# A second junk buffer for the squares of a set-attention and SoLU kernel

## The chip, the cores and the metric

One core of one Trainium2 chip. The metric is the device time of one launch in microseconds; lower is better. The engines are named as the profile names them: PE (TensorE, matmuls; PEld its weight loads), DVE (VectorE), ACT (ScalarE), POOL (GpSimd), SP (SyncE, which issues the DMAs).

## The reference

`x` has 4 sets of 12608 tokens of 128 channels. An attention with 32 inducing points makes `h` per set, a second one lets the tokens attend to `h`; its 50432 rows then go through a feed-forward part of width 1024:

```python
def mab(q, kv):
    s = scale * (q @ kv.transpose(0, 2, 1))
    a = np.exp(s - s.max(-1, keepdims=True))
    a /= a.sum(-1, keepdims=True) + 1e-09
    return a @ kv
h = mab(I, x)
out = mab(x, h)
...
h = x @ w_in
e = np.exp(h - np.max(h, axis=-1, keepdims=True))
solu = h * (e / (np.sum(e, axis=-1, keepdims=True) + 1e-09))
mu, var = mean(solu), mean((solu - mu) ** 2)
ln = (solu - mu) / np.sqrt(var + 1e-06) * g_ln
return ln @ w_out
```

## The kernel before

The tokens of a set are cut into tiles of 128, four to a group, 396 tiles in all. A tile of the feed-forward part runs through `soft` (L1337): PE has put the 1024 columns of `h` into PSUM (L1276, L1306), DVE copies them, scaled by the attention's norm, into a buffer `hn` and takes their extreme (L1349); ACT takes the exponential into a buffer `eu` and its sum into a column of `qe` (L1360); POOL multiplies the two in place, which gives solu without its norm (L1364, 2.37 us each); then two engines read `eu`: ACT squares it for the variance (`square`, L1373 to L1382, its instruction on L1375), and DVE transposes it in blocks into `vt` (L1391). PE multiplies `vt` by the output weights in a stream of small matmuls (`emit` in `products`, L1551), DVE or ACT moves the sums out of PSUM (`evacuate`, L1580), and `finish` (L1605 to L1630) turns the sums into the norm and scales the rows. Pieces of one tensor, `spare`, serve as further buffers for `hn`, `eu` and results, so some rows name `spare` where others name `eu` or `hn`.

The square's 128x1024 result is needed by nobody: only its sum is, which the instruction hands to a column of `qe` as its accumulated output (a second record in the trace, ACTIVATION_READ_ACCUMULATOR). The result itself goes to a junk buffer in bf16, `sq` (L340), one for the whole kernel. A buffer `eu` is free again when its square and its transposition are both done.

A planner written in Python (`Planner`, `Op`, costs in ns, priorities such as `PR_SQ`) sets the order of each engine's instructions at build time. It knows nothing of waits on `sq`: the cost it takes for a square is 1040 ns, whatever stands ahead. Each engine then works its list in that order. The framework adds the waits: every ACT instruction counts up one semaphore, shown as Activation_49; an instruction that writes what an earlier one has written or read waits for that count, also on its own engine. A wait that an earlier wait of the same engine already covers is left out. An instruction holds one wait; for a second one an EVENT_SEMAPHORE instruction is put ahead of it.

Of the kernel before, what the change touches and what calls it, by code (L numbers as in the profile page):

```python
# [10 lines left out]
BF16 = mybir.dt.bfloat16  # L11
U32 = mybir.dt.uint32
I32 = mybir.dt.int32
AF = mybir.ActivationFunctionType
# [5 lines left out]
P = 128  # L20
C = 128
M = 32
FF = 1024
# [16 lines left out]
OS_LATE = 2000  # L40
SLOTS = 3
STRETCH = 20
JS = [
# [56 lines left out]
PR_SQ = 6  # L100
# [59 lines left out]
class Planner:  # L160
# [8 lines left out]
    def spawn(self, gen, prio):  # L169
        self._step([gen, prio, 0], None)  # L170
# [8 lines left out]
    def give(self, lock, buf, *after):  # L179
        lock.free.append((buf, after))  # L180
        while lock.free and lock.waiting:
            lock.waiting.sort(key=lambda w: (w[2], w[1]))
            task = lock.waiting.pop(0)[0]
            self.blocked -= 1
            self._step(task, lock.free.pop(0))
# [69 lines left out]
    def run(self):  # L255
        clock = self.clock
        while self.ops:
            first = min(self.ops, key=lambda o: (max(clock[o[0].eng], o[1]), o[3]))
            eng = first[0].eng
            limit = max(clock[eng], first[1]) + self.slack[eng]  # L260
            stretch = int(limit / 1000 / STRETCH)
            wide, turn = JS[stretch] if stretch < len(JS) else (0, 0)
            pick = min(
# [20 lines left out]
def set_attention_then_solu_kernel(ctx: ExitStack, tc: tile.TileContext, x, inducing, w_in, w_out, g_ln, out):  # L284
    nc = tc.nc
    NB, N, _ = x.shape
    scale = 1.0 / float(C) ** 0.5
# [27 lines left out]
    def buf(shape, name, dtype=F32, where=None):  # L315
        return (where or const).tile(shape, dtype, name=name)

    def bufs(n, shape, name, dtype=F32):
        return [buf(shape, f"{name}{i}", dtype) for i in range(n)]
# [17 lines left out]
    where = bank_pool.__enter__()  # L337
    bank_e = [buf([P, 512], f"bank_e{i}", where=where) for i in range(8)]
    hn_b = bufs(3, [P, FF], "hn")
    sq = buf([P, FF], "sq", BF16)  # L340

    eu_b = buf([P, EUS, FF], "eu")
    xT_b = buf([C, PG, P], "xT")
# [996 lines left out]
    def soft(t, b, j, s, hp, d):  # L1340
        G = grp[(b, j)]
        ka, i = part_of[b, ff_groups[j][0] + s]
        A = aT_of[(b, ka)]
        hn, rel = yield HN
        nm, mrel = yield NM
        rn = A["aT"][1][:, i : i + 1]
        d = yield Op(
            "DVE", 1208,
            lambda: nc.vector.tensor_scalar(out=hn, in0=hp, scalar1=rn, scalar2=None, op0=ALU.mult, op1=ALU.min, accum_out=nm),  # L1349
            d, rel, mrel, prio=t + PR_HN,  # L1350
        )
        give(H, hp, d)
        give(TURN, None, d)
        A["left"] -= 1
        if not A["left"]:
            give(AT, A["aT"], d)
        srel = yield G["st"]
        e, rel = yield EU
        de = yield Op(
            "ACT", 1133, lambda: nc.scalar.activation(e, hn, AF.Exp, bias=nm, scale=-1.0, accum_out=G["qe"][:, s, 1:2]), d, rel, srel,  # L1360
            prio=t + PR_EX,
        )
        give(NM, nm, de)
        d = yield Op("POOL", 2330, lambda: nc.gpsimd.tensor_tensor(out=e, in0=hn, in1=e, op=ALU.mult), de, prio=t + PR_MU)  # L1364
        give(HN, hn, d)
        left = []

        def over(d):
            left.append(d)
            if len(left) == 2:  # L1370
                give(EU, e, *left)

        def square():  # L1373
            ds = yield Op(
                "ACT", 1040, lambda: nc.scalar.activation(sq, e, AF.Square, scale=1.0 / 32.0, accum_out=G["qe"][:, s, 0:1]), d,  # L1375
                prio=t + PR_SQ,
            )
            G["squared"].append(ds)
            over(ds)
            if (b, j) != final and len(G["squared"]) == ff_groups[j][1]:  # L1380
                yield from floor(b, j)

        spawn(square(), t)
        n = ff_groups[j][1]
        rel = yield G["vt"]
        if (b, j) == final:
            yield from straight(t, b, j, s, e, d, rel, over)
            return
        dt = yield Op(
            "DVE", 1163,  # L1390
            lambda: nc.vector.transpose(  # L1391
                out=G["vtb"][:, : n * FF].rearrange("p (j s t) -> p j s t", j=M, s=n)[:, :, s, :],
                in_=e.rearrange("p (a f) -> p a f", f=M),
            ),
            d, rel, prio=t + PR_TU,
        )
        over(dt)
        G["turned"].append(dt)
        if len(G["turned"]) == n:
            for w in range(2):  # L1400
                spawn(products(b, j, t, w), t)

    def floor(b, j):
        G = grp[(b, j)]
        n = ff_groups[j][1]
        flat = G["dd"][: P * 2 * n].rearrange("(p f) -> p f", f=2 * n)
        ds = yield dma(
            P * 8 * n, lambda: nc.sync.dma_start(flat, G["qe"][:, :n, :].rearrange("p s v -> p (s v)")), G["squared"], prio=-30, issue=600
        )
        f, i = fin_of[b, j]  # L1410
        F = fin[(b, f)]
        rel = yield F["buf"]
        dl = F["dl"][:, 4 * i : 4 * i + 4, :]
        laid = G["dd"][: P * 2 * n].rearrange("(a t s v) -> s t a v", a=4, t=M, v=2)
        dealt = []
        for s in range(n):
            d = yield dma(P * 8, lambda: nc.sync.dma_start(dl[s * M : (s + 1) * M], laid[s]), ds, rel, prio=-30, issue=600)
            dealt.append(d)
        plan.set(G["floor"], *dealt)
        give(ST, G["stb"], *dealt)  # L1420
# [14 lines left out]
    def straight(t, b, j, s, e, d, vrel, over):  # L1435

        G = grp[(b, j)]
        f, _ = fin_of[b, j]
        F = fin[(b, f)]
        uT = G["vtb"].rearrange("p (s k t) -> p s k t", s=GS, k=KC)[:, s]  # L1440
        tr, rel = yield H.at(OP_FIRST + t)

        def turn():
            for k in range(KC):
                nc.tensor.transpose(out=tr[:, k * P : (k + 1) * P], in_=e[:, k * P : (k + 1) * P], identity=ident)

        d = yield Op("PE", SWITCH + 108.7 * KC, turn, d, rel, prio=t - 60)
        over(d)
        half = KC // 2
        view = tr.rearrange("p (k t) -> p k t", k=KC)  # L1450
        halves = []

        def part(eng, cost, fn, k0):
            dc = yield Op(eng, cost, lambda: fn(uT[:, k0 : k0 + half], view[:, k0 : k0 + half]), d, vrel, prio=t - 60)
            halves.append(dc)
            if len(halves) == 2:
                plan.set(turned_both, *halves)

        turned_both = Event()
        spawn(part("ACT", 510, nc.scalar.copy, 0), t - 60)  # L1460
        spawn(part("DVE", 620, nc.vector.tensor_copy, half), t - 60)
        got = yield turned_both
        give(H, tr, *got)
        wrel = yield w_full_ready
        bank, rel = yield H.at(OP_FIRST + t)

        def add():
            for k in range(KC):
                nc.tensor.matmul(bank[:, : C + 1], lhsT=uT[:, k], rhs=w_full[0][:, k], start=(k == 0), stop=(k == KC - 1))

        d = yield Op("PE", SWITCH + 225 * KC, add, got, rel, wrel, prio=t - 55)
        rel = yield F["buf"]
        d = yield Op("ACT", 190, lambda: nc.scalar.copy(F["raw"][:, s, :], bank[:, : C + 1]), d, rel, prio=t - 60)
        give(H, bank, d)
        F["out"].append(d)
        F["left"] -= 1
        if not F["left"]:
            spawn(last_finish(b, j, f), -100)
# [282 lines left out]
```

## Time and profile before

| | before |
|---|---|
| median of 3 runs (lowest to highest) | 1186.43 us (1186.13 to 1186.9) |
| the profiled execution's own time | 1184.99 us |
| its span, first to last instruction | 1183.1 us |
| granted TensorE clock, mean | 0.996 |
| squares on ACT (L1375) | 329 + 67 |

Times and busy shares are of one profiled execution. A row of the time line gives an instruction's start in us from the span's start, its length in us, engine, line, operation, what it writes and reads, its shape, and how many such instructions in a row it stands for. An instruction of ACT may start before the record ahead of it has ended.

### The profile page before, as it was taken

What the parts mean: (1) busy time and instruction counts of PE and PEld (TensorE: products, weight loads), DVE (VectorE), ACT (ScalarE), POOL (GpSimd) and SP (SyncE); (2) the same over time, 40 slices, a digit from 0 to 9 for tenths busy, and PEclk for the clock granted to TensorE, in tenths of its full rate; (3) what the DMA queues carried; (4) which work ended last, traced back from release to release, by engine and by line L of the source; (5) the groups of instructions that cost most, each with busy time, mean ns of one, the idle gap of its engine ahead of it and who ended that gap; (6) DMA issues with size and microseconds to landing.
All of it is one profiled execution on the core that took longest, in us unless ns stands there. A gap on an engine that the chain in (4) does not pass through costs nothing.

```text
span 1183.1 us, 67935 instructions
## 1 busy us (share of the span) xinstructions
PE 1147.1 (97%) x30537; PEld 1050.5 (89%) x30537; DVE 1073.7 (91%) x1628; ACT 1115.4 (94%) x2193; POOL 1064.2 (90%) x619
## 2 busy tenths in 40 slices
PE   9899999999999999999999999999999999999996
PEld 7568999998999898989899989999899989899896
DVE  6899999998999899999999899999999998999891
ACT  4799999999999999999999999999999999999994
POOL 2488899988998999989899899899999999999995
PEclk9999999999999999999999999999999999999999
DMA  9632332432144333423122354242313132120203
GB/s 337 238 118 75 111 111 76 136 96 67 25 117 119 108 111 110 129 81 100 40 58 83 96 147 151 75 126 61 84 40 84 41 80 67 31 65 4 49 5 88
DMA packets 167108, 110.62 MB, mean 93 GB/s; under 512 B 78336, under 2 KB 132000, under 8 KB 166688
## 3 DMA queue, kind: packets, MB, share of 16 engines
q1 hardware_dynamic: 166816, 106.27, 31.1%
q8 instruction: 239, 3.92, 1.4%
q14 instruction: 53, 0.43, 0.1%
HBM read 53.51 MB, written 52.17 MB: 89 GB/s over the span
## 4 chain that ended last, share of the span: by engine, by line
PE 39%; ACT 31%; POOL 11%; issue 7%; DVE 7%; DMA 3%; SPq 0%; ACTq 0%; DVEq 0%; POOLq 0%
PE h L1551 30%; ACT sq L1375 12%; ACT eu L1360 11%; POOL eu L1364 8%; PE h L1306 3%; ACT spare L1360 2%; POOL spare L1364 2%; DVE vt L1391 2%; DVE spare L1349 2%; ACT spare L1580 1%; DVE hn L1349 1%; POOL spare L1626 1%; ACT a L1048 1%; ACT xT L700 1%; PE h L688 1%
## 5 line engine op out<-in xcount | busy, mean ns | idle before, releaser
L1551 PE MATMUL h<-wc,vt 32*128 32x129 f32 (+1 forms) x25344 | 986.7, 273 | 12.9 <-ACT spare L1580 7.9
L1551 PEld LDWEIGHTS h<-wc,vt 32*128 32x128 f32 (+1 forms) x25344 | 954.9, 184 | 44.7 <-ACT spare L1580 17.5
L1364 POOL TENSOR_TENSOR eu<-hn,eu 128x1024 f32<-128x1024 f32 x166 | 392.7, 2373 | 26.9 <-ACT eu L1360 25.7
L1306 PE MATMUL h<-hs,aT 32*128 32x512 f32 x1528 | 404.9, 602 | 4.9 <-DVE hn L1349 1.4
L1391 DVE STREAM_TRANSPOSE vt<-eu 128x1024 f32<-128x1024 f32 x326 | 398.3, 1231 | 12.1 <-POOL eu L1364 11.1
L1364 POOL TENSOR_TENSOR eu<-spare,eu 128x1024 f32<-128x1024 f32 x163 | 385.7, 2373 | 19.4 <-ACT eu L1360 19.2
L1375 ACT ACTIVATE sq<-eu 128x1024 bf16<-128x1024 f32 x329 | 345.6, 1050 | 13.9 <-POOL eu L1364 5.8
L1349 DVE TENSOR_SCALAR_CACHE_REDUCE hn<-h,rn 128x1024 f32<-128x1024 f32 x201 | 253.2, 1261 | 21.6 <-PE h L1306 10.1
L1349 DVE TENSOR_SCALAR_CACHE_REDUCE spare<-h,rn 128x1024 f32<-128x1024 f32 x195 | 245.7, 1263 | 22.4 <-PE h L1306 9.6
L1360 ACT ACTIVATE eu<-hn,nm 128x1024 f32<-128x1024 f32 x166 | 189.1, 1139 | 1.9 <-DVE hn L1349 1.3
L1360 ACT ACTIVATE eu<-spare,nm 128x1024 f32<-128x1024 f32 x163 | 185.9, 1141 | 2.2 <-DVE spare L1349 1.8
L1306 PEld LDWEIGHTS h<-hs,aT 32*128 32x128 f32 x1528 | 121.7, 185 | 22.2 <-issue 3.9
L1364 POOL TENSOR_TENSOR spare<-spare 128x1024 f32<-128x1024 f32 x32 | 75.9, 2371 | 9.2 <-ACT spare L1360 8.9
L1391 DVE STREAM_TRANSPOSE vt<-spare 128x1024 f32<-128x1024 f32 x66 | 81.4, 1233 | 2.6 <-POOL spare L1364 2.5
L1364 POOL TENSOR_TENSOR spare<-hn,spare 128x1024 f32<-128x1024 f32 x35 | 83.0, 2372 | 0.0
L1626 POOL TENSOR_TENSOR spare<-spare,fin 128x512 f32<-128x512 f32 x79 | 79.7, 1039 | 1.6
L1375 ACT ACTIVATE sq<-spare 128x1024 bf16<-128x1024 f32 x67 | 70.3, 1049 | 1.9 <-POOL spare L1364 0.3
L1375 ACT ACTIVATION_READ_ACCUMULATOR sq<-eu 128x1 f32 x329 | 61.8, 188 | 0.0
L688 PE MATMUL h<-ident,xn 32*128 32x32 f32 x1124 | 51.4, 224 | 0.9 <-issue 0.6
L1580 ACT COPY spare<-h 128x774 f32<-128x774 f32 (+3 forms) x69 | 45.0, 654 | 6.0 <-PE h L1551 4.0
L688 PEld LDWEIGHTS h<-ident,xn 32*128 32x128 f32 x1124 | 49.0, 136 | 1.3 <-issue 0.8
L1360 ACT ACTIVATE spare<-hn,nm 128x1024 f32<-128x1024 f32 x35 | 39.9, 1140 | 0.1
(200 smaller groups left out, 935.7 us busy)
## 6 DMA issues: line engine op xcount, KB each, us to landing
out_dram<-spare SPq DMA_DIRECT2D x95, 256.0 KB, 3.1
xT<-xd SPq DMA_DIRECT2D x93, 256.0 KB, 3.9
xn<-in_x_dram SPq DMA_DIRECT2D x75, 256.0 KB, 3.8
xd<-xT SPq DMA_DIRECT2D x72, 256.0 KB, 2.7
dl<-dd SPq DMA_DIRECT2D x392, 1.0 KB, 2.7
xd<-vt SPq DMA_DIRECT2D x7, 768.0 KB, 7.9
spare<-in_x_dram SPq DMA_DIRECT2D x15, 256.0 KB, 7.6
wc<-in_x_dram SPq DMA_DIRECT2D x6, 256.0 KB, 4.1
```

Source lines behind the costliest of these rows:

```text
L688: nc.tensor.transpose(out=tr[:, k * 512 + s * M : k * 512 + (s + 1) * M], in_=xn[r, s, :], identity=ident[r, r])
L700: lambda: nc.scalar.copy(xT.rearrange("c s (q t) -> c q s t", q=4)[:, 2 * w : 2 * w + 2, :n, :], tr.rearrange("c (k x) -> c k x", k=2)[:, ...
L1048: de = yield Op("ACT", 90 + 54 * n, lambda: nc.scalar.activation(a4[:, :n], twice, AF.Exp, scale=scale), d, arel)
L1306: nc.tensor.matmul(hp[:, cols], lhsT=aT[rows, i // 2, :], rhs=hs[rows, cols], start=True, stop=True)
L1349: lambda: nc.vector.tensor_scalar(out=hn, in0=hp, scalar1=rn, scalar2=None, op0=ALU.mult, op1=ALU.min, accum_out=nm),
L1360: "ACT", 1133, lambda: nc.scalar.activation(e, hn, AF.Exp, bias=nm, scale=-1.0, accum_out=G["qe"][:, s, 1:2]), d, rel, srel,
L1364: d = yield Op("POOL", 2330, lambda: nc.gpsimd.tensor_tensor(out=e, in0=hn, in1=e, op=ALU.mult), de, prio=t + PR_MU)
L1375: "ACT", 1040, lambda: nc.scalar.activation(sq, e, AF.Square, scale=1.0 / 32.0, accum_out=G["qe"][:, s, 0:1]), d,
L1391: lambda: nc.vector.transpose(out=G["vtb"][:, : n * FF].rearrange("p (j s t) -> p j s t", j=M, s=n)[:, :, s, :], in_=e.rearrange("p (a f) ...
L1551: nc.tensor.matmul(op[:rows, a - 2 * w, :], lhsT=vt[q, k, :], rhs=wc[q, k, :], start=(k == 0), stop=(k == JB - 1))
L1580: return lambda: eng(to, at)
L1626: return lambda: eng.tensor_tensor(out=raw, in0=raw, in1=y[:, i0 : i0 + 4].unsqueeze(2).to_broadcast([rows, 4, C]), op=ALU.mult)
```

## The change

Two junk buffers `sq0` and `sq1` stand in the place of `sq`, and the squares, in the order in which the planner places them, take them in turn. The planner's cost for a square is the same number under a name. The second buffer takes 2 KB of every partition and lies behind the first, so all tensors allocated later move by 2 KB.

```diff
+SQ_NS = 1040
...
-    sq = buf([P, FF], "sq", BF16)
+    sq_b = bufs(2, [P, FF], "sq", BF16)
+    squares = [0]
...
         def square():
-            ds = yield Op(
-                "ACT", 1040, lambda: nc.scalar.activation(sq, e, AF.Square, scale=1.0 / 32.0, accum_out=G["qe"][:, s, 0:1]), d,
-                prio=t + PR_SQ,
-            )
+            def squared():
+                squares[0] += 1
+                nc.scalar.activation(sq_b[squares[0] % 2], e, AF.Square, scale=1.0 / 32.0, accum_out=G["qe"][:, s, 0:1])
+
+            ds = yield Op("ACT", SQ_NS, squared, d, prio=t + PR_SQ)
```

The instructions of all five engines stand in the same order in both programs, and on PE, DVE, POOL and SP every wait is for the same count of the same semaphore. Only waits of ACT for its own semaphore differ. In the rows that follow, a number behind a tile's name is a running number of the build (`sq_83` is `sq0` and `sq_84` is `sq1` in the changed program), Activation_49 is ACT's own semaphore and Pool_49 that of POOL; line numbers of the changed program are two or three higher.

ACT, the piece of its list that the trace has at 263 to 271 us, before:

```order
L1360 ACTIVATE eu,qe_104<-spare,nm_114 128x1024
L1612 ACTIVATE fin_109<-fin_109 128x20 [waits Pool_49]
L1613 ACTIVATE fin_109<-fin_109 128x20 [waits Activation_49]
L1614 ACTIVATE fin_109<-fin_109 128x20 [waits Activation_49]
L1375 ACTIVATE sq,qe_102<-eu 128x1024
L1375 ACTIVATE sq,qe_104<-eu 128x1024 [waits Activation_49,Pool_49]
L1375 ACTIVATE sq,qe_104<-eu 128x1024 [waits Activation_49]
L1375 ACTIVATE sq,qe_104<-eu 128x1024 [waits Activation_49,Pool_49]
L1618 ACTIVATE fin_109<-fin_109 128x20 [waits Pool_49]
```

The same piece of the changed program:

```order
L1362 ACTIVATE eu,qe_105<-spare,nm_115 128x1024 [waits Activation_49]
L1615 ACTIVATE fin_110<-fin_110 128x20 [waits Pool_49]
L1616 ACTIVATE fin_110<-fin_110 128x20 [waits Activation_49]
L1617 ACTIVATE fin_110<-fin_110 128x20 [waits Activation_49]
L1378 ACTIVATE sq_83,qe_103<-eu 128x1024
L1378 ACTIVATE sq_84,qe_105<-eu 128x1024 [waits Pool_49]
L1378 ACTIVATE sq_83,qe_105<-eu 128x1024 [waits Activation_49]
L1378 ACTIVATE sq_84,qe_105<-eu 128x1024 [waits Activation_49,Pool_49]
L1621 ACTIVATE fin_110<-fin_110 128x20 [waits Pool_49]
```

Nothing moved. Before, the second, third and fourth instruction in a row that squares waits for the count of the square just ahead of it. After, the second square has lost that wait, and the waits for Activation_49 of the third and the fourth are for the square two places ahead, which wrote the same junk buffer. The exponential in the first row has gained a wait for a count that an earlier square's wait covered before.

ACT, the piece at 277 to 281 us, before (the square ahead of the first COPY is the one that the second square waits for):

```order
L1375 ACTIVATE sq,qe_106<-eu 128x1024 [waits Pool_49]
L1580 COPY spare<-h_698 128x2x3x129 [waits PE_49]
L1375 ACTIVATE sq,qe_106<-spare 128x1024 [waits Activation_49,Pool_49]
L1580 COPY spare<-h_696 128x2x3x129 [waits PE_49,Activation_49]
L950 ACTIVATE accn<-acc_128,small_120 128x128 [waits DVE_49]
```

The same piece of the changed program:

```order
L1378 ACTIVATE sq_84,qe_107<-eu 128x1024 [waits Pool_49]
L1583 COPY spare<-h_699 128x2x3x129 [waits PE_49]
L1378 ACTIVATE sq_83,qe_107<-spare 128x1024 [waits Pool_49]
L1583 COPY spare<-h_697 128x2x3x129 [waits PE_49,Activation_49]
L952 ACTIVATE accn<-acc_129,small_121 128x128 [waits DVE_49]
```

Nothing moved here either; the second square has lost a wait for the square two places ahead.

Counted over the whole list of ACT: 142 of the 396 squares stand directly behind another square and wait for it before; 52 of them have that wait alone, 90 have one for POOL too. In the changed program no square waits for the instruction directly ahead of it. Of the 142, 87 wait for a square two or more places ahead and 55 have no wait for ACT left. 65 exponentials that had no wait for ACT's own semaphore have one: 9 of them for the square two places ahead, 56 for one three or more places ahead. 29 exponentials wait for the square directly ahead of them in both programs, since they overwrite the `eu` that it reads.

## Rows read from the trace of the kernel before

**Rows 1.** The page's first lines: span, and busy time of each engine.

```profile
span 1183.1 us, 67935 instructions
PE 1147.1 (97%) x30537; PEld 1050.5 (89%) x30537; DVE 1073.7 (91%) x1628; ACT 1115.4 (94%) x2193; POOL 1064.2 (90%) x619
```

**Rows 2.** Busy time by stretch: us, then busy us by engine with instruction counts.

```profile
core 0: us, PE busy (x) PEld busy (x) DVE busy (x) ACT busy (x) POOL busy (x), PEclk, DMA share, GB/s
...
900.00:1000.00 100.00, 97.04 (x2754) 91.42 (x2750) 96.53 (x128) 97.96 (x190) 98.95 (x55) 1.00 0.22 52
...
1100.00:1160.00 60.00, 57.55 (x1585) 54.88 (x1582) 49.10 (x62) 58.17 (x121) 59.84 (x37) 1.00 0.15 34
...
100.00:1160.00 1060.00, 1040.18 (x28882) 969.76 (x28878) 988.85 (x1436) 1032.27 (x2015) 997.58 (x567) 1.00 0.30 82
```

**Rows 3.** Longest waits of ACT from 100 to 1160 us: us, times, longest us.

```profile
ACT sq L1375 <- POOL eu L1364: 2.6, 8, 0.5
ACT xT L700 <- PE h L688: 2.2, 4, 1.4
```

**Rows 4.** Waits of POOL and of PE's weight loads for ACT, whole span.

```profile
POOL eu L1364 <- ACT eu L1360: 44.9, 36, 5.5
...
PEld h L1551 <- ACT spare L1580: 17.5, 25, 1.7
```

**Rows 5.** The chain that ended last, shares by engine, then by line.

```profile
PE 39%; ACT 31%; POOL 11%; issue 7%; DVE 7%; DMA 3%; SPq 0%; ACTq 0%; DVEq 0%; POOLq 0%
...
by line: PE h L1551 29.8%; ACT sq L1375 12.4%; ACT eu L1360 10.7%; POOL eu L1364 8.3%; issue 7.1%; PE h L1306 3.5%; ACT spare L1360 2.0%; POOL spare L1364 1.9%; DVE vt L1391 1.7%; DVE spare L1349 1.5%; ACT spare L1580 1.4%; DVE hn L1349 1.3
```

**Rows 6.** The chain by line, from 300 to 400, then from 900 to 1000 us.

```profile
by line: PE h L1551 65.1%; PE h L1306 7.3%; ACT eu L1360 7.0%; ACT sq L1375 6.1%; issue 5.2%; PE h L768 2.0%; ACT xT L700 1.9%; PE h L1093 1.3%; ACT spare L1580 1.1%; ACT a L1048 1.0%; PE h L885 0.9%; PE h L688 0.9%; PE h L806 0.6%; ACT spa
...
by line: ACT sq L1375 26.4%; ACT eu L1360 26.3%; issue 12.8%; PE h L1551 7.9%; ACT spare L1360 6.9%; DVE vt L1391 3.6%; DVE spare L1349 3.4%; ACT spare L1580 2.3%; ACT a L1048 1.9%; DMA dl<-dd 1.7%; DMA dd<-qe 1.4%; DVE hn L1349 1.3%; DVE s
```

**Rows 7.** Time line of ACT: a square with no late wait, and four in a row.

```profile
238.62 1.04 ACT L1375 ACTIVATE sq<-eu 128x1024 bf16<-128x1024 f32 x1
239.57 0.19 ACT L1375 ACTIVATION_READ_ACCUMULATOR sq<-eu 128x1 f32 x1
239.66 1.13 ACT L1360 ACTIVATE eu<-hn,nm 128x1024 f32<-128x1024 f32 x1
...
264.90 1.04 ACT L1375 ACTIVATE sq<-eu 128x1024 bf16<-128x1024 f32 x1
265.85 0.19 ACT L1375 ACTIVATION_READ_ACCUMULATOR sq<-eu 128x1 f32 x1
266.13 1.06 ACT L1375 ACTIVATE sq<-eu 128x1024 bf16<-128x1024 f32 x1
...
267.31 1.06 ACT L1375 ACTIVATE sq<-eu 128x1024 bf16<-128x1024 f32 x1
...
268.55 1.06 ACT L1375 ACTIVATE sq<-eu 128x1024 bf16<-128x1024 f32 x1
...
269.61 0.20 ACT L1618 ACTIVATE fin<-fin 128x20 f32<-128x20 f32 x1
```

**Rows 8.** Groups of squares: count, busy us, mean ns, idle us before them.

```profile
L1375 ACT ACTIVATE sq<-eu 128x1024 bf16<-128x1024 f32 x329 | 345.6, 1050 | 13.9 <-POOL eu L1364 5.8
...
L1375 ACT ACTIVATE sq<-spare 128x1024 bf16<-128x1024 f32 x67 | 70.3, 1049 | 1.9 <-POOL spare L1364 0.3
```

**Rows 9.** Time line of ACT: a square with two waits behind a COPY.

```profile
278.91 0.81 ACT L1580 COPY spare<-h 128x774 f32<-128x774 f32 x1
279.62 1.06 ACT L1375 ACTIVATE sq<-spare 128x1024 bf16<-128x1024 f32 x1
```

**Rows 10.** The line L1375 alone: its extra wait instructions, ns min/median/max.

```profile
L1375 ACTq EVENT_SEMAPHORE  x171: 17/17/17, 84.0 to 1163.6; - x171
```

## The prediction

> **What bounds the kernel now.** I read the busy shares first, then the waits, then the chain that ended last, and only then the squares. All four computing engines are nearly full: over the span ACT is busy 94% of the time, DVE 91%, POOL 90%, and PE shows 97% [rows 1]. From 100 to 1160 us, where the feed-forward part runs steadily, ACT is busy 1032.27 of 1060 us, PE 1040.18, POOL 997.58, DVE 988.85 [rows 2]. So the question is which of them sets the pace. The waits say that ACT hardly waits for anyone: its two longest sorts of wait in that stretch come to 2.6 and 2.2 us [rows 3], though it is idle for 1060 - 1032.27 = 27.7 us. The others do wait for ACT: POOL 44.9 us for the exponentials, PE's weight loads 17.5 us for the copies out of PSUM [rows 4]. That idle time of ACT that no other engine ends is the first hint that ACT waits for itself. The chain that ended last runs 39% on PE and 31% on ACT, with POOL at 11% and DVE at 7%; the squares alone hold 12.4% of it [rows 5]. It changes hands: from 300 to 400 us the matmul stream of L1551 holds 65.1%, and from 900 to 1000 us squares and exponentials hold 26.4 + 26.3% [rows 6].
>
> **What a square's wait costs.** The reader should compare starts. A square that is followed by an instruction without a late wait passes the engine on after 239.66 - 238.62 = 1.04 us: the exponential starts 0.10 us before the square's accumulator record has ended (239.57 + 0.19 = 239.76) [rows 7]. In the run of four squares, the second starts at 266.13, which is 0.09 us after the first one's record has ended (265.85 + 0.19 = 266.04); the distances from start to start are 1.23 (two waits), 1.18 (one wait) and 1.24 us (two waits), and the last square takes 269.61 - 268.55 = 1.06 us until L1618 starts [rows 7]. The order of the program says why: each of these squares waits for the count of the one ahead, since both write `sq`. So a wait for the square directly ahead costs 1.18 - 1.04 = 0.14 us where it stands alone and 1.24 - 1.04 = 0.20 us where POOL's wait makes a second one. In both figures 0.02 us is the square's own longer run to its accumulator record, 1.06 us against 1.04.
>
> **The sum on ACT.** 142 squares have such a wait, 52 alone and 90 with a second one: 52 x 0.14 + 90 x 0.20 = 7.3 + 18.0 = 25.3 us of ACT's time. The change takes all 142 away, since the square directly ahead now writes the other buffer. As a check, the profile puts 13.9 + 1.9 us of idle time before squares, and lays only 5.8 + 0.3 us of it to POOL [rows 8]; the rest is the waiting, and the lost overlap is not idle time and so is not in that figure.
>
> **What is added.** 87 of the 142 squares now wait for a square two or more places ahead. A full square of 1.04 us lies between, so that wait should be over before the engine is free. The row that is nearest is a square that in the old program waits for the square two places ahead and for POOL: it starts at 279.62, 0.10 us before the COPY ahead of it ends (278.91 + 0.81 = 279.72) [rows 9]. I cost these at nothing; the cover is the square between. The 65 exponentials that gain a wait for a square two or more places ahead are costed at nothing by the same row; if the cover failed, each would pay between 0.14 and 0.20 us, 9 to 13 us in all. The extra wait instructions take 17 ns each on ACT's sequencer [rows 10] and run ahead of the engine; squares need fewer of them, exponentials more, so the balance is nothing. The order on every engine is unchanged, and no other engine waits for a square except by way of a free `eu` buffer and the small DMAs of the sums, which can only come earlier. The 2 KB move of the later tensors changes no shape and no start within a row; I cost it at nothing.
>
> **What of it reaches the end.** Only squares on the path that sets the end can shorten it. The squares hold 12.4% of 1183.1 us, 146.7 us, of the chain [rows 5], out of 345.6 + 70.3 = 415.9 us that they are busy [rows 8]. So 146.7 / 415.9 = 35% of them lie on the chain, and 0.35 x 25.3 = 8.9 us leave it. The bounds are nothing, if PE or POOL is just as late wherever ACT is on the chain, and 25.3 us, if ACT sets the pace throughout. I take 8.0: the figure of the chain less a tenth, because another path of nearly the same length is late next where the chain changes engines, above all POOL, which is busy 98.95 of 100 us from 900 and 59.84 of 60 us from 1100 [rows 2].
>
> **A rule that speaks against it.** The trace has ACT's next instruction start 0.10 us early without a late wait and 0.09 us late with one [rows 7]. The Trainium skill, VectorE: DVE Perf Modes, section The DRAIN you can't avoid, says of VectorE that its emptying of the pipeline cannot be skipped by leaving out semaphores between operations, and that the semaphore costs nothing extra. By that rule, were it true of ACT, the sum would be nothing. The rows of this trace say otherwise for ACT, so it keeps a small chance, as the third rival.
>
> **The rivals.** First, *ACT sets the pace throughout*. For it: ACT waits so little for others [rows 3], and PE's share of the chain rests on ends of matmuls that the profile models. The whole 25.3 us would come off, less what POOL, full at the end [rows 2], keeps back: 12 to 23 us, about 16, so some 1170 us. Against it: the chain leaves ACT for 69% of the time [rows 5]. The Trainium skill, Perfetto Trace Analysis, section Identifying the Most-Contended Engine, holds matmul busy time to be a poor measure and points to the weight loads; by that reading ACT's 94% would be the highest here, above the weight loads' 89%, which is this rival.
>
> Second, *PE is late next*. If its 1040.18 us are real work, it has 1060 - 1040.18 = 19.8 us left [rows 2], of which 31%, ACT's part of the chain [rows 5], is 6.1 us; some of that PE waits for DVE and for its own issue. A gain of 0 to 4 us, about 2, so some 1184 us. For it: the stretch from 300 to 400 us, where the stream of L1551 holds the chain [rows 6]. Against it: the weight loads' waits for ACT [rows 4], which would shrink.
>
> Third, *a square behind a square cannot start earlier anyway*, because the accumulator record must be out first: no change, 1186.4 us. Against it: the exponential at 239.66, which starts before that record has ended [rows 7], and which writes an accumulator too.
>
> Fourth, on the other side, *the waits move to the exponentials*. If 65 of them pay 0.20 us, that is 13.0 us; exponentials stand ahead of POOL, which waits for them already [rows 4]. Were all of that on the chain and the squares' gain hidden, the result would be 1199 us. It turns slower from 8.9 / 0.20 = 45 late waits on the chain. Against it: the square of [rows 9], and that each of them waits for an instruction at least two places ahead.
>
> **How the numbers follow.** The sum is made against the profiled execution, 1184.99 us with a span of 1183.1 us [rows 1]; the median of the runs is 1.4 us above that, and I subtract from the median: 1186.43 - 8.0 = 1178.4 us. A measurement of this kernel can tell about 0.2%, 2.4 us, from no change. The forecast, a gain of 4 to 12 us, has a chance of 0.60; ACT throughout 0.16; PE next 0.18, of which 0.05 would be within 2.4 us; no earlier start 0.03; the exponentials 0.03. Faster is 0.60 + 0.16 + 0.13 = 0.89, the same 0.05 + 0.03 = 0.08, slower 0.03. The range runs from a gain of 15 us to one of 2 us, 1171.4 to 1184.4 us: it leaves out about 0.06 of the first rival, 0.05 of the second, and the last two, 0.17 together.
>
> **What would show it.** Right: squares in a row start 1.04 us apart, no square takes 1.06 us for that reason, the idle time before squares falls to the part that POOL ends, the exponentials keep their 0.10 us early start, and the new idle time of ACT is put down to PE, DVE or POOL. Starts still 1.18 or more apart would make the price wrong; starts 1.04 apart with the end hardly moved would make the share of the chain wrong, and the rows would then show which engine ACT waits for.

## The result and the profile after

The changed kernel takes 1170.12 us (median of 4 runs, 1169.5 to 1171.28) against 1186.66 us (median of 4 runs, 1186.13 to 1186.93): a ratio of 0.9862 with a 95% interval of 0.9845 to 0.9879. That is 16.5 us less, about twice the forecast, and below the range. Two later comparisons of the same kernel on other occasions gave 0.9879 and 0.9864.

Span and busy time of the profiled execution after (1171.28 us), to set against [rows 1], and its chain that ended last, to set against [rows 5]:

```profile
span 1169.5 us, 67905 instructions
PE 1143.9 (98%) x30537; PEld 1049.5 (90%) x30537; DVE 1071.5 (92%) x1628; ACT 1102.5 (94%) x2193; POOL 1064.1 (91%) x619
...
PE 46%; POOL 20%; ACT 17%; DVE 8%; issue 6%; DMA 3%; SPq 1%; ACTq 0%; DVEq 0%; POOLq 0%
```

ACT's share of the chain fell from 31% to 17%, POOL's rose from 11% to 20%. ACT's busy time fell by 12.9 us: in the lost overlap the square's accumulator record ran with nothing beside it, so it counted as busy ([rows 7]: the record ends at 266.04, the next square starts at 266.13). The rest of what was removed was idle time, as the groups of squares show below.

The time line of ACT after, in the piece of the program that [rows 7] show before:

```profile
262.74 1.04 ACT L1378 ACTIVATE sq<-eu 128x1024 bf16<-128x1024 f32 x1
263.69 0.19 ACT L1378 ACTIVATION_READ_ACCUMULATOR sq<-eu 128x1 f32 x1
263.78 1.04 ACT L1378 ACTIVATE sq<-eu 128x1024 bf16<-128x1024 f32 x1
...
264.82 1.04 ACT L1378 ACTIVATE sq<-eu 128x1024 bf16<-128x1024 f32 x1
...
265.86 1.04 ACT L1378 ACTIVATE sq<-eu 128x1024 bf16<-128x1024 f32 x1
...
266.90 0.20 ACT L1621 ACTIVATE fin<-fin 128x20 f32<-128x20 f32 x1
```

The four squares now start 1.04 us apart and all take 1.04 us; from the first one's start to L1621 it is 4.16 us, where it was 269.61 - 264.90 = 4.71. That is 0.55 us less for one wait of 0.14 and two of 0.20, as priced. The third and fourth still wait for the square two places ahead, and that costs nothing here. What holds for this run of four holds for the list: read over the whole trace, the 52 squares with one wait started at the median 1.17 us after the square ahead and the 90 with two 1.24 us; after the change the median of the 142 is 1.04 us.

The groups of squares after, to set against [rows 8]:

```profile
L1378 ACT ACTIVATE sq<-eu 128x1024 bf16<-128x1024 f32 x329 | 343.7, 1045 | 7.1 <-POOL eu L1366 6.5
...
L1378 ACT ACTIVATE sq<-spare 128x1024 bf16<-128x1024 f32 x67 | 70.0, 1046 | 0.5 <-POOL spare L1366 0.5
```

The line's extra wait instructions after, to set against [rows 10]:

```profile
L1378 ACTq EVENT_SEMAPHORE  x93: 17/17/17, 96.7 to 1147.9; - x93
```

The idle time before squares fell from 13.9 + 1.9 to 7.1 + 0.5 us, and nearly all that is left, 6.5 + 0.5, is ended by POOL. So the part that POOL does not end fell from 9.7 to 0.6 us. With the 12.9 us of busy time that makes 22.0 us, near the 25.3 us priced. The squares need 93 extra wait instructions in place of 171.

Who waited after: ACT for POOL in the steady part (100 to 1150 us), then POOL and the weight loads for ACT over the span, to set against [rows 3, 4]:

```profile
ACT sq L1378 <- POOL eu L1366: 5.4, 14, 1.2
...
POOL eu L1366 <- ACT eu L1362: 38.6, 32, 5.5
...
PEld h L1554 <- ACT spare L1583: 12.5, 21, 1.3
```

Busy time by stretch after, with the columns of [rows 2]:

```profile
900.00:1000.00 100.00, 98.01 (x2774) 93.07 (x2771) 95.46 (x126) 97.85 (x192) 99.84 (x58) 1.00 0.24 56
...
1087.00:1147.00 60.00, 58.23 (x1549) 55.49 (x1541) 47.60 (x60) 56.41 (x116) 59.84 (x38) 0.97 0.15 35
```

Both waits for ACT shrank: POOL's from 44.9 to 38.6 us, the weight loads' from 17.5 to 12.5. ACT's waits for POOL before squares rose from 2.6 to 5.4 us, and POOL is busy 99.84 of 100 us from 900 and 59.84 of 60 us near the end. All of ACT's waits for other engines together, from 100 to 1150 us, rose from 14.3 to 23.2 us (the view counts gaps over 0.15 us): those for POOL by 4.2 us, for PE by 2.2 and for DVE by 2.5. This is about what is missing between the 25.3 us that ACT was spared and the 16.5 us that came out. PE, with the same instructions, is idle by the profile for 1169.5 - 1143.9 = 25.6 us in place of 1183.1 - 1147.1 = 36.0.

### The profile page after: what moved, and what is told of

It reads as the page before. It is cut to its first block, busy times and chain, and to the rows that moved or that the text cites. A ratio compares the mean times of both kernels' runs of the same rounds, so it can differ in the third digit from the quotient of the medians.

```text
span 1169.5 us, 67905 instructions
## 1 busy us (share of the span) xinstructions
PE 1143.9 (98%) x30537; PEld 1049.5 (90%) x30537; DVE 1071.5 (92%) x1628; ACT 1102.5 (94%) x2193; POOL 1064.1 (91%) x619
## 4 chain that ended last, share of the span: by engine, by line
PE 46%; POOL 20%; ACT 17%; DVE 8%; issue 6%; DMA 3%; SPq 1%; ACTq 0%; DVEq 0%; POOLq 0%
PE h L1554 35%; POOL eu L1366 13%; ACT sq L1378 6%; ACT eu L1362 6%; PE h L1308 4%; POOL spare L1366 3%; POOL spare L1629 3%; DVE vt L1394 2%; DVE spare L1351 2%; DVE hn L1351 1%; PE h L1028 1%; ACT spare L1583 1%; ACT spare L1362 1%; DMA hs<-in_moe_w_out_dram 1%; PE h L690 1%
## 5 line engine op out<-in xcount | busy, mean ns | idle before, releaser
L1351 DVE TENSOR_SCALAR_CACHE_REDUCE spare<-h,rn 128x1024 f32<-128x1024 f32 x195 | 245.5, 1262 | 21.1 <-PE h L1308 10.9
```

## The experiments

Two theories stood against each other. **Theory 1**: the chain that ended last bounds the gain, and only my count of the waits on it was wrong. **Theory 2**: ACT sets the pace nearly throughout, also where the chain is drawn along PE.

**The place of the tensors.** The second buffer moves every later tensor by 2 KB. This kernel has the move alone:

```diff
-                nc.scalar.activation(sq_b[squares[0] % 2], e, AF.Square, ...)
+                nc.scalar.activation(sq_b[0], e, AF.Square, ...)
```

> Both junk buffers are allocated, so every later tensor lies 2 KB further on, but all squares still write the first one, and all 142 waits for the square directly ahead stay. If the gain of 16.5 us comes from the removed waits (both the theory that ACT sets the pace and the theory that the profile's chain decides), the time is that of before, 1186.7 us within 2. If the place of the tensors is what gains, it is near 1170.

Ratio 1.001 (0.9996 to 1.0023), with every wait of the kernel before in place. Its idle time before the squares that read `eu` is the old one:

```profile
L1378 ACT ACTIVATE sq<-eu 128x1024 bf16<-128x1024 f32 x329 | 345.7, 1051 | 13.9 <-POOL eu L1366 5.8
```

So the place of the tensors gives nothing; the gain is the waits'.

**The waits on the chain alone, and the others alone.** The squares keep their buffer, except that it changes at the squares named in a set, so that only these lose their wait for the square directly ahead. The set holds, by running number, the 64 squares of which the profile's chain of before runs through the square ahead, the wait and the square itself; in the second kernel, the other 78.

```diff
+TURNS = {
+    12, 37, 41, 42, 44, 45, 46, 53, 58, 60, 61, 62, 65, 66, 82, 83, 84, 86, 102, 105,
...
-    squares = [0]
+    squares = [0, 0]
...
                 squares[0] += 1
-                nc.scalar.activation(sq_b[squares[0] % 2], e, ...)
+                squares[1] ^= squares[0] in TURNS
+                nc.scalar.activation(sq_b[squares[1]], e, ...)
```

> The buffer changes only at 64 of the 142 squares: those whose wait for the square directly ahead lies on the chain that ended last in the profile of before, by price 64 waits worth 11.2 us of the 25.3 us of ACT's time. Theory 1, the chain decides and only my count of it was wrong (share of busy time in place of a count of waits): a gain of 9 to 11 us, about 1176.5. Theory 2, ACT sets the pace nearly throughout, wherever the chain is drawn: a gain in proportion to ACT's time, 16.5 x 11.2 / 25.3 = 7.3 us, about 1179.4.

> The other half: the buffer changes only at the 78 squares whose wait does not lie on that chain, worth 14.0 us of ACT's time. Theory 1 (the chain decides): no more than 0 to 2 us, 1185 to 1187, since the chain stays as long as it was. Theory 2 (ACT sets the pace): 16.5 x 14.0 / 25.3 = 9.2 us, about 1177.5.

> The changed kernel once more, on the chip of the three runs beside it, so that their gains can be set against it: 1170 us, ratio 0.985 to 0.988 by both theories.

On one chip: the waits on the chain 0.9923 (0.9904 to 0.9943), the others 0.9947 (0.9928 to 0.9966), both together 0.9879 (0.9862 to 0.9897). Of the 1185.7 us of before these are gains of 9.1, 6.3 and 14.3 us. Theory 1 falls: waits that do not lie on the chain gave 6.3 us alone, with an interval from 4.0, where a path that truly set the end would have given nothing. Theory 2 in its plain form does not fit well either: in proportion to ACT's time it gives 14.3 x 11.2 / 25.3 = 6.3 and 14.3 x 14.0 / 25.3 = 7.9 us, within the second interval and just short of the first, which begins at 6.8, and in the other order. A us of waiting was worth 9.1 / 11.2 = 0.8 us on the chain and 6.3 / 14.0 = 0.45 us off it, though the intervals of the two (0.60 to 1.02 and 0.29 to 0.61) just touch. So the chain seems to rank waits; it does not bound what they are worth.

**PE with less to do.** If PE does not bound the stretches in which the chain lies on it, less work for PE must leave the time alone. Both kernels leave out every eighth step of the product stream, so their outputs lack that part of the sum.

```diff
         def emit(a, k):
+            if k % 8 == 3:
+                return
             q = slice(a * M, (a + 1) * M)
```

> The kernel before, with every eighth step of the product stream left out (k = 3, 11, 19, 27 of 32; the output is not the reference's): 3168 of 25344 matmul records of L1551 go, about 396 beats of 0.224 us, 89 us of PE's time. Theory 1, PE is the bound where the chain lies on it: L1551 holds 30% of the chain, 353 us, and an eighth of that is 44 us, so a gain of 20 to 44 us. Theory 2, PE's part of the chain hides waits for ACT and the rest, and ACT sets the pace: a gain of 0 to 8 us.

> The changed kernel with the same eighth of the product stream left out. Against the run beside it, this gives what the second junk buffer is worth when PE has 89 us less to do. Theory 1: PE kept back most of the 25.3 us, so with PE eased the change is worth 20 to 25 us. Theory 2: little more than with PE whole, 14 to 18 us, since POOL and DVE keep back the rest.

Before with less PE work: 0.9957 (0.9941 to 0.9974), 5.1 us faster for what the expectation estimates as 89 us less of PE's work. The change with less PE work: 0.9816 (0.9786 to 0.9845). The two differ by 0.0141 of 1185.4 us, 16.7 us, about what the change gives with PE whole. Busy time of before with less PE work, to set against [rows 1], its chain, its stream beside that of the kernel before (L1551), and its busy time by stretch from 100 to 300 us, with the columns of [rows 2]:

```profile
PE 1113.5 (94%) x27369; PEld 988.7 (84%) x27369; DVE 1073.4 (91%) x1628; ACT 1113.2 (94%) x2193; POOL 1064.3 (90%) x619
...
ACT 48%; POOL 17%; issue 11%; PE 10%; DVE 6%; DMA 5%; SPq 2%; ACTq 0%; DVEq 0%; POOLq 0%
...
L1551 PE MATMUL h<-wc,vt 32*128 32x129 f32 (+1 forms) x25344 | 986.7, 273 | 12.9 <-ACT spare L1580 7.9
...
L1553 PE MATMUL h<-wc,vt 32*128 32x129 f32 (+1 forms) x22176 | 944.1, 277 | 20.3 <-ACT spare L1582 13.9
...
100.00:300.00 200.00, 190.41 (x4780) 170.76 (x4777) 184.21 (x282) 191.07 (x371) 177.43 (x101) 0.97 0.33 93
```

PE's share of the chain drops from 39% to 10%, and the time moves little: another path, along ACT, was nearly as long all the time. PE waits for ACT more instead: 13.9 us ahead of the stream's matmuls, 7.9 before. Of the 89 us the profile shows 33.6 as less busy time of PE and 61.8 as less of its weight loads.

Part of the gain is hidden by the granted TensorE clock: its mean was 0.986 of full speed in the profiled execution, and 0.97 from 100 to 300 us, against 0.996 and 1.00 before. At the same mean clock of 0.991, three runs with less PE work took 1178.2 to 1178.5 us and two runs of the kernel before 1186.6 and 1188.9, so the gain is then 8 to 11 us. That is just over the edge of what theory 2 allowed and well short of the 20 to 44 us of theory 1. The 16.7 us above is some 3 us too high for the same reason: at 0.991 and 0.990 (one run) the two kernels with less PE work lie 13 us apart. With PE eased the change is thus worth no more than with PE whole, where theory 1 had 20 to 25 us.

**A little more work for one engine.** The last group adds 132 short instructions to one engine, on a small buffer of their own, so that nothing else waits for them. What comes out of the added time tells how far that engine sets the pace. For ACT after the change:

```diff
                 nc.scalar.activation(sq_b[squares[0] % 2], e, AF.Square, ...)
+                padded[0] += 1
+                if padded[0] % 3 == 0:
+                    nc.scalar.copy(pad[:, padded[0] // 3 % 4, :], ident[:, :8])
```

In the kernel before the copy stands behind every third exponential, since behind a square it would stand in the waits that are in question. POOL gets `nc.gpsimd.tensor_tensor(out=pad[...], in0=ident[:, :8], in1=ident[:, :8], op=ALU.mult)` behind every third product, DVE `nc.vector.tensor_copy(pad[...], ident[:, :8])` behind every third scaling.

> The changed kernel with a copy of 8 columns into a small buffer of its own behind every third square: 132 short ACT instructions of about 0.11 us from start to start, 14 to 16 us more for ACT, and no wait on any other engine. Theory 2 (ACT still sets the pace after the change): 0.5 to 0.8 of that comes out, 8 to 12 us slower than the changed kernel. Theory 1 (the pace has passed to PE and POOL): under 0.3 of it, 0 to 4 us.

> The changed kernel with a product of 8 columns into a small buffer behind every third product of POOL: 132 short instructions of some 0.1 to 0.15 us, 13 to 20 us more for POOL. Theory 2: under 0.3 of it comes out. Theory 1: 0.3 to 0.6 of it.

> The kernel before, with a copy of 8 columns behind every third exponential: 132 short ACT instructions, by the run of the changed kernel 0.087 us each from start to start, 11.5 us more for ACT. Theory 2 (ACT sets the pace before the change, nearly throughout): 0.6 to 0.9 of it comes out, 7 to 10 us slower than before. Theory 1 (ACT only where the profile's chain lies on it, 31%): 0.31 x 11.5 = 3.6 us slower, at most 5.

> The kernel before, with a product of 8 columns behind every third product of POOL, 132 x 0.160 = 21.1 us more for POOL. In the changed kernel this made 9 to 11 us. If ACT set the pace before and POOL is what keeps back the rest of the 25.3 us since, it makes much less here, 2 to 6 us. If POOL was as late before as it is now, 9 to 11 us again.

> The changed kernel with a copy of 8 columns behind every third scaling of DVE: 132 short DVE instructions of some 0.07 to 0.1 us, 9 to 13 us more for DVE. DVE holds 8% of the chain after the change: 0 to 3 us slower than the changed kernel if that is its share; 4 us or more if DVE is among the engines that set the pace now.

> The changed kernel on the chip of the three runs beside it, as their base: a ratio of 0.985 to 0.989 to before by either theory.

The added instruction itself, on ACT (first two rows) and on POOL (the others), each time with the one that follows it (in the kernel before the view of waits puts 8.2 us of POOL's waiting down to the copy, but the program has POOL wait for the exponential ahead of it):

```profile
940.05 0.18 ACT L1383 COPY pad<-ident 128x8 f32<-128x8 f32 x1
940.14 1.27 ACT L1638 ACTIVATE spare<-spare,fin 128x128 f32<-128x128 f32 x4
```

```profile
960.40 0.20 POOL L1372 TENSOR_TENSOR pad<-ident 128x8 f32<-128x8 f32 x1
960.56 2.39 POOL L1369 TENSOR_TENSOR eu<-hn,eu 128x1024 f32<-128x1024 f32 x1
```

It holds ACT for 0.09 us (0.087 at the median), 11.5 us for 132, and POOL for 0.16 us, 21.1 us for 132. The outcome. The base of the two rows of the change is the changed kernel's 0.9879, taken on the same chip in the comparison before; that of the other two is the kernel before:

| more work for | ratio to before (95% interval) | against its base | of the added time |
|---|---|---|---|
| ACT, kernel before | 1.0071 (1.0051 to 1.0092) | +8.4 us | 0.73 |
| ACT, change | 0.9928 (0.9904 to 0.9953) | +5.8 us on 0.9879 | 0.50 |
| POOL, kernel before | 1.0047 (1.003 to 1.0063) | +5.6 us | 0.26 |
| POOL, change | 0.9962 (0.9948 to 0.9976) | +9.8 us on 0.9879 | 0.46 |

Before, 0.73 of what ACT gets more comes out, far over the 0.31 of the chain; theory 2 had said 0.6 to 0.9. The interval allows 0.5 to 0.95, and a part is the granted clock: at a mean clock of 0.991 the runs took 1193.3 and 1194.1 us against 1187.2 of before, some 6.5 us or 0.57. After, neither theory holds alone. POOL's part is higher, 0.46, as theory 1 had it; ACT's 5.8 us lie between the 0 to 4 and the 8 to 12 us forecast, and its lower share is not clear of the noise. So the change hands part of the pace to POOL. POOL keeps back part of the rest of the 25.3 us; by ACT's waits above, PE and DVE do so too.

The run with more work for DVE gave 1.0771 (1.0706 to 1.0836), far beyond either expectation, and says nothing of DVE's part in the pace: the copies took 1.1 us each on average in place of under 0.1 (last section).

## Why the prediction was wrong, point by point

- **The price of a wait, right.** 0.14 and 0.20 us, 25.3 us on ACT; the run of four squares shortened by 0.55 us where 0.54 was priced, and over the whole list the medians were 1.17 and 1.24 us, then 1.04.
- **Nothing added, right.** The waits two places ahead and those of the exponentials cost nothing that shows: squares with such a wait start 1.04 us apart, and the idle time before squares is nearly all ended by POOL. The 65 exponentials that gained a wait have 0.4 us of idle time ahead of them all together, 0.5 before.
- **What reaches the end, wrong.** The step that failed reads: "So 146.7 / 415.9 = 35% of them lie on the chain, and 0.35 x 25.3 = 8.9 us leave it." Two things were wrong in it. The smaller is that it took the squares' share of busy time for the share of the waits: counted one by one, 64 of the 142 lie on the chain, 11.2 of 25.3 us, 44%. The larger is that it took the chain for a bound: "Only squares on the path that sets the end can shorten it." 16.5 of the 25.3 us came out, 65% (14.3, 57%, in the smallest of the three comparisons, which lies inside the range but, like the others, above the forecast of 4 to 12); the 78 waits off the chain gave 6.3 us alone; and PE, which held 39% of the chain, could be relieved of an estimated 89 us for 5.1, or 8 to 11 at equal clock. The 64 waits on the chain alone gave 9.1 us, near the 8.9 of the prediction; that is chance, since the prediction had them worth 8.9 us and they were worth 11.2. The tenth that I took off for what is late next named POOL, which is indeed one of the engines late next, but it stood on the wrong base.
- **The first rival came nearest.** "ACT sets the pace throughout", a gain of 12 to 23 us, about 16, had a chance of 0.16. Throughout is too much, since 0.6 to 0.7 of added ACT time came out and 0.26 of added POOL time; and its 16 was no sum, so that the number fits is in part luck. What spoke for it was in the rows: ACT's waits for others of 2.6 and 2.2 us in 1060 [rows 3], against the waits of POOL and the weight loads for ACT [rows 4]. Those two are the longest sorts only: all together, from 100 to 1160 us, ACT waits 14.6 us for others, so about 13 of its 27.7 us of idle time are ended by no other engine. In the same view PE's matmuls wait 18.2 us, 12.7 of them for ACT, POOL 60.3, 54.9 of them for ACT, and DVE 65.0. So ACT and PE wait for others about equally little; what sets ACT apart is that the others' waits are for it, and I let the chain outvote that. By the reading of the Trainium skill, Perfetto Trace Analysis, section Identifying the Most-Contended Engine, ACT was the most contended engine. The runs agree: most of the added ACT time came out.
- **The other rivals fell.** "PE is late next" by the gain itself, 14 us and more where it allowed 4, and by the run with less PE work; "no earlier start" by the starts 1.04 us apart; "the waits move to the exponentials" by the total.
- **Open.** Why the chain is drawn along PE where PE can be relieved with little gain. The profile models the ends of matmuls, so a short wait of PE can lie hidden under the matmul ahead; this was not shown. DVE's part in the pace was not measured either. Two things were not tried: a third buffer, for which no room is left in SBUF, and more `eu` buffers against the 29 exponentials that still wait for the square directly ahead.

## What to carry to other kernels

An output that nobody reads still makes its writer wait for the one ahead if both go to one buffer; on an engine that is busy 97% of the time, look at the starts of equal instructions in a row, with and without such a wait, and give junk a second buffer. Ask for the bound by who waits for whom before by the chain: in this kernel the engine that waited little for others, and that PE and POOL waited for, set most of the pace, and the chain, through engines that are all about 90% busy or more, was one of several of nearly the same length. Where it matters, add a known 10 us to one engine and see how much comes out, and compare runs at the same granted clock.

## What the hardware showed that I had not expected

A wait for the instruction directly ahead costs ACT more than the lost overlap: a square that waits so also takes 0.02 us longer to its accumulator record (all 142 did; but 1.06 us is not peculiar to it, the square of [rows 9] takes it without a late wait), and a second wait, for a POOL product, adds 0.06 us, though POOL ends only 5.8 + 0.3 us of the idle time before squares [rows 8], and though two waits cost nothing where neither is late [rows 9]. The trace puts the extra wait instruction of the square at 266.13 at 266.07, only after the record ahead has ended at 266.04; where the wait is not late, it stands well ahead, at 264.95 for the square at 265.86 of the changed program.

Most of DVE's short copies in the run with more work for DVE lasted until a POOL instruction ended. Their group, in the view of groups, then their durations in ns (min/median/max) by tile:

```profile
L1355 DVE COPY pad<-ident 128x8 f32<-128x8 f32 x132 | 151.6, 1149 | 0.0
...
L1355 DVE COPY pad<-ident x132: 157/1118/6992, 53.8 to 1250.2; 128x8 f32<-128x8 f32 x132
```

One of them and the DVE instruction behind it, then the POOL product of that time, in the time line:

```profile
500.08 2.02 DVE L1355 COPY pad<-ident 128x8 f32<-128x8 f32 x1
502.02 0.67 DVE L1137 TENSOR_REDUCE nr<-a 128x16 f32<-128x512 f32 x1
...
499.70 2.38 POOL L1370 TENSOR_TENSOR eu<-hn,eu 128x1024 f32<-128x1024 f32 x1 [0.58 <-ACT eu L1366]
```

The copy of 8 columns runs from 500.08 to 502.10, the product from 499.70 to 502.08. Of the 132 copies, 106 took over 0.3 us, and each of these ended 0.02 to 0.04 us after a POOL instruction. All 132 take 151.6 us, and the kernel became 1280.78 us long. DVE's scalings and transpositions of 1024 columns show no such thing beside the same products. The Trainium skill, SBUF — State Buffer, section Who interferes with whom, says that copies can take both of DVE's port pairs and then exclude GpSimd, and that the one that comes second is blocked for the whole instruction of the other; this row agrees. Two copies were held through several products on end, which goes beyond one instruction: the longest, from 1165.71, took 6.99 us.

```profile
1165.71 6.99 DVE L1355 COPY pad<-ident 128x8 f32<-128x8 f32 x1
...
1165.68 2.39 POOL L1370 TENSOR_TENSOR eu<-spare,eu 128x1024 f32<-128x1024 f32 x1
1168.01 2.37 POOL L1370 TENSOR_TENSOR eu<-hn,eu 128x1024 f32<-128x1024 f32 x1
1170.31 2.36 POOL L1370 TENSOR_TENSOR eu<-spare,eu 128x1024 f32<-128x1024 f32 x1
```
